# An attention and MoE kernel on one core: dependent operations moved one step back, loads in one ring, a second PSUM bank for P·V

## The chip, the cores and the metric

One core of a Trainium2 chip runs the whole program. The time is the device time of one execution in microseconds (us); the profile is of one further execution.

## The reference

Three stages follow each other. Attention with a decay term is computed for 4 batches of 8 heads, 576 tokens and 64 channels; then a dense layer with a hard-swish gate; then a layer in which each of the 2304 tokens goes to one of 8 experts.

```python
scores = q @ k.T / sqrt(D) + (cum[i] - cum[j])      # cum = cumsum(log f), causal
attn   = softmax(scores);  x = attn @ v             # 4 x 8 x 576 x 64 -> 2304 x 512
h = x @ w_in;  g = h * clip(h + 3, 0, 6) / 6;  x = g @ w_out      # 512 -> 2048 -> 512
e = argmax(x @ w_gate)                               # one of 8 experts per token
out = gate_prob * sigmoid(x @ w_output_gate)[e] * (relu(x @ w1[e]) @ w2[e])   # 512 -> 1024 -> 512
```

## The kernel before

Every matrix product runs as three 16-bit products. An operand is split into a high half (a copy by ACT) and a low half (the difference, by POOL or DVE). So nearly every operand passes an ACT instruction and then a POOL or DVE instruction before TensorE (PE) can use it.

**Attention.** `plan` (L543 to L565) lists the steps of the attention, 37 or 38 in batches 1 to 3. ("p", b, n) prepares a piece n of k and q: `split_kq` (L207) has ACT and POOL split it, SP issues DMA transposes (L269, L285, L288), and a copy of the rows to other partitions (L242 on ACT; L240 on DVE in the first batch) is put off by COPY_LAG scored steps (`copy_rows`, `flush_copies`), or until the step that needs it (`flush_for`). ("v", b, t) prepares a block of v (`prep_v`: ACT L333, POOL L334). The others score a head against a block of queries: `score` (L340: PE L312, then DVE L358 or L384), one step later `soft` (L389: ACT exp L392 and copy L409 or L413, POOL L410 or L415, DMA transpose L421 of the probabilities, tile pt), and LAG = 4 steps later `pv` (L525: PE L444 to L459 into one PSUM bank, tile pv, then `evac` and `evac_last` by DVE L467 to L485 into xs, and ACT and POOL into xn). Two heads share a bank, and the next pair of heads waits until DVE has emptied it. DMA transposes (L507) make xT, the input of the dense layer. The loads of k, q and v have one buffer each (tags ldk, ldq, ldv): those of k and q are issued when the piece before has been split, and that of v inside `prep_v`, just ahead of its use.

**Dense layer.** 6 chunks of 384 tokens. `moe1_steps` (L697) yields 32 parts a chunk: 16 of 12 matmuls into h (L709; then ACT L716, DVE L717, ACT L719, DVE L722, with three PSUM banks in turn), then 4 by 4 parts of 12 matmuls from g (L734; then ACT L743 and DVE L744). The loop over the chunks (L1111) puts attention steps between the parts, by a pace (`want`), so that the attention of later chunks is done beside the dense layer of earlier ones. In this loop the order on PE, ACT and DVE is the order of the program; SP and POOL are ordered by the framework's scheduler.

**Work put between the parts.** The weights of the dense layer arrive as 64-bit floats; `conv_raw` (L661) makes two 16-bit halves of a piece of 512 KB: DVE L672, L674, L676, then ACT L679, then POOL L680. 18 of 32 pieces are converted before the loop, 14 in the first chunk at the parts CONV_AT, and each conversion is followed by `load_next` on SP's queue, for a buffer that the conversion two before it has emptied. Their PSUM bank (ps_cv) is given back after the last of them. `gate_steps` (L792) is the gating of a finished chunk, run from the next chunk's loop at parts 3, 5 and 7. `weights_steps` (L863) converts the first experts' weights (ACT L898, DVE L899) at the even parts of the last two chunks, from `open_weights` on, which first runs the attention to its end. The end of `attn_seq` is one step: `drain(0)` does the last four P·V products and, when it comes to the last unit, that unit's softmax.

**Experts.** From 660 us on the experts run; the diff changes only the order of a few gating steps there.

Of the kernel before, what the change touches and what calls it, by code (L numbers as in the profile page):

```python
# [18 lines left out]
P = 128  # L19
# [12 lines left out]

COPY_LAG = 2

LEAD = 2

LAG = 4
# [23 lines left out]
def attention_moe_kernel(ctx: ExitStack, tc: tile.TileContext, q, k, v, f, w_in, w_out,  # L61
# [112 lines left out]
    def load(i, which):  # L174

        if i >= B * NTB:
            return
        for nm in which:
            with tc.issue_after(gate[0]) if gate else nullcontext():
                if i < (3 if nm == "v" else PE_PIECES):  # L180
                    t = spare(i if nm == "v" else 3 + 2 * i + "kq".index(nm)).bitcast(F32)
                else:
                    t = ap1.tile([P, H * D], F32, tag=f"ld{nm}", name=f"ld{nm}", bufs=1)
                if nm == "v":
                    b, tb = i // NTB, i % NTB
                    r = TBR[tb]
                    src = v[b, :, tb * 128:tb * 128 + r, :].rearrange("h p d -> p h d")
                    for e in range(128 // r):
                        nc.sync.dma_start(out=t[e * r:e * r + r].rearrange("p (h d) -> p h d", d=D), in_=src)
                    t = t.rearrange("p (h d) -> p h d", d=D)  # L190
                else:
                    b, r, hs, (nh, n), cs = piece(i)
                    src = (k if nm == "k" else q)[b, hs, cs, :].rearrange("h (p c) d -> p h (c d)", c=n)
                    nc.sync.dma_start(out=t[0:r].rearrange("p (h x) -> p h x", h=nh), in_=src)
                    t = t.rearrange("p (n d) -> p n d", d=D)
                ld[i, nm] = t

    def load_cum(b, hh):
# [8 lines left out]
    def split_kq(nm, i):  # L207

        b, r, hs, (nh, n), cs = piece(i)
        t = ld.pop((i, nm))  # L210
        p = split_tile(nm, i)
        tv = t[0:r].rearrange("p (h c) d -> p c h d", h=nh) if nm == "k" else t[0:r]
        hi, lo = (p[0:r, :, x] for x in ((0, 1) if nm == "k" else (1, 0)))
        if nm == "k":
            hi, lo = (a.rearrange("p (c h) d -> p c h d", h=nh) for a in (hi, lo))
        nc.scalar.activation(out=hi, in_=tv, func=AF.Copy)
        nc.gpsimd.tensor_tensor(out=lo, in0=tv, in1=hi, op=ALU.subtract)
        return p[0:r].rearrange("p n c d -> p (n c d)")

# [98 lines left out]
    def prep(b, n):  # L318
        i = b * NTB + n
        prep_k(i)  # L320
        if i > 3:
            load(i + 1, "k")
        prep_q(i)
        if i > 3:
            load(i + 1, "q")

    def prep_v(b, tb):
        if b * NTB + tb > 2:
            load(b * NTB + tb, "v")
        assert all(u[1] == b for u in pend)  # L330
        tv, V = ld.pop((b * NTB + tb, "v")), vt[b % len(vt)]
        r = TBR[tb]
        nc.scalar.activation(out=V[:, tb, :, 0:64], in_=tv, func=AF.Copy)  # L333
        nc.gpsimd.tensor_tensor(out=V[0:r, tb, :, 65:129].bitcast(BF16), in0=tv[0:r], in1=V[0:r, tb, :, 0:64],  # L334
                                op=ALU.subtract)


# [173 lines left out]

    cur = {}
    late = []
# [31 lines left out]
    for b in range(B):  # L545
# [19 lines left out]
        ends.append(len(plan) - 1)  # L565
    pend = []
    complete = []

    def attn_seq():

        def drain(n):
            while len(pend) > n:
                u = pend.pop(0)
                if u in unsoft:
                    soft(u)
                    unsoft.remove(u)
                pv(u)

# [25 lines left out]
        for it in plan:  # L604
            if it == "drain":
                drain(0)
                finish(9)
                load(4, "kq")
            elif it[0] == "p":
# [18 lines left out]
            yield "end"  # L628
        drain(0)
        finish(9)  # L630
        yield "end"

# [4 lines left out]
    raws = {}  # L637
    last_act = []
    wof = wo.rearrange("p a b c -> p (a b c)")
# [20 lines left out]

    def conv_raw(nm, i):  # L661

# [15 lines left out]
        tf = t.bitcast(F32).rearrange("p (a b) -> p a b", a=4)  # L678
        last_act.append(nc.scalar.activation(out=hi, in_=tf, func=AF.Copy).ins)  # L679
        nc.gpsimd.tensor_tensor(out=lo.bitcast(BF16), in0=tf, in1=hi, op=ALU.subtract)  # L680

# [110 lines left out]
    def gate_steps(c):  # L792
# [46 lines left out]
        nc.vector.tensor_reduce(out=sx, in_=t2, axis=AX.X, op=ALU.add)  # L839
        nc.scalar.activation(out=z, in_=z, func=AF.Exp, scale=-1.0)  # L840
# [3 lines left out]
        nc.vector.tensor_reduce(out=rank[:, bs].unsqueeze(2), in_=t4, axis=AX.X, op=ALU.add)  # L844
        nc.vector.tensor_scalar(out=z, in0=z, scalar1=1.0, scalar2=None, op0=ALU.add)
        nc.vector.tensor_scalar(out=sx, in0=sx, scalar1=1e-9, scalar2=None, op0=ALU.add)
# [16 lines left out]
    def weights_steps(wp):  # L863
# [28 lines left out]
        for i, (_, e, which, js) in enumerate(parts):  # L892
# [169 lines left out]
    def load_next(queue):  # L1062
        if not loads:
            return
        nm, i = loads[0]

        if ((nm, i - 8) if nm == "wi" else (nm, same_room(i))) in conv:
            return
        loads.pop(0)
        after = gate  # L1070
        with tc.issue_after(after[-1]) if after else nullcontext():
            load_raw(nm, i, queue)
# [23 lines left out]
    goals = [ends[need[c + 1] - 1] + 1 + LAG + XLAG for c in range(NCH - 1)]  # L1096
    mp2 = None
    gq = []
    wg_ = None
# [3 lines left out]
    def open_weights():  # L1103
        nonlocal wp, wg_
        while adv():
            pass
        attn_ctx.close()
        wp = ctx.enter_context(tc.tile_pool(name="wp", bufs=1, side="right"))
        wg_ = weights_steps(wp)

    for c in range(NCH):  # L1111
# [14 lines left out]
        for part in moe1_steps(c):  # L1126
# [9 lines left out]
            while nsteps[0] < want and adv():  # L1136
                pass
            if c == 0 and k_ == GATE_LOAD:
                load_gates()
            if conv and k_ == CONV_AT[2 * NF - EARLY_CONV_DONE - len(conv)]:  # L1140
                assert conv[0] not in loads
                conv_raw(*conv.pop(0))
                load_next(nc.sync)
                if not conv:
                    stage_ctx.close()
                    mp2 = moe1_ctx.enter_context(tc.tile_pool(name="mp2", bufs=1))
                    setup_gates()
            if gq and k_ in (3, 5, 7):
                run(gq[0])
                if k_ == 7:  # L1150
                    run(gq.pop(0))
            if c == NCH - 2 and wp is None and len(complete) == 3 * B:
# [19 lines left out]
        gq.append(gate_steps(c))  # L1172
    run(wg_, 4 * KD + 1 - nw)
    main.close()
    ET = mybir.EngineType
# [6 lines left out]
    run(first[0], 2)  # L1182
    run(last, 2)
    run(first[0], 3)
    run(last, 2)
    count_rounds()
# [100 lines left out]
```

## Time and profile before

| | |
|---|---|
| median of 3 runs | 891.51 us |
| lowest and highest | 888.04 and 895.68 us |
| the profiled execution | 894.32 us, its span 892.6 us |
| mean granted TensorE clock | 0.935 |

The time of a row is counted from the start of the span. Idle time of an engine stands in brackets with what ended it, its releaser. The granted clock is a share of 2.4 GHz; the lower level is 1.2 GHz, so a stretch with a mean of 0.75 was at the lower level half of the time. SPq rows are DMA issues by SP; their duration is that of the issue, not of the transfer.

### The profile page before, as it was taken

How to read it: one execution, taken by the hardware profiler on the slowest of the kernel's cores; microseconds unless marked ns; L12 is line 12 of the kernel's file. 1: busy time of each engine (PE TensorE's matmuls, PEld its weight loads, DVE VectorE, ACT ScalarE, POOL GpSimd, SP SyncE). 2: the span in 40 equal slices, each digit the busy share in tenths (PEclk: the TensorE clock that was granted, in tenths of full speed). 3: DMA queues.
4: the chain of work that ended last, by engine and by line, in shares of the span. 5: the costliest groups of instructions: out<-in, count | busy, mean ns of one | idle time of the engine just before them, and what ended most of it. 6: DMA issues, size and time to landing. Idle time of an engine off the chain costs nothing. (4 is left out here: it accounts for less than half of the span.)

```text
span 892.6 us, 16737 instructions
## 1 busy us (share of the span) xinstructions
PE 749.2 (84%) x6177; PEld 481.4 (54%) x6177; DVE 460.9 (52%) x1272; ACT 456.4 (51%) x909; POOL 306.5 (34%) x388
## 2 busy tenths in 40 slices
PE   4744696666999989997799897976999999999994
PEld 3532354343566556664456554643576866766651
DVE  7896866343754364357333861467232455554510
ACT  4854566553776576457555762444011455554520
POOL 8345545552454344343344441000003222221011
PEclk9967898897999999999899997999899999999997
DMA  9558477784668777477448564532325699887410
GB/s 250 152 172 184 108 115 159 163 165 101 137 116 146 131 122 145 89 138 128 95 90 152 90 110 127 174 109 95 95 59 144 145 262 264 272 268 227 156 47 35
DMA packets 263778, 127.95 MB, mean 143 GB/s; under 512 B 214658, under 2 KB 247522, under 8 KB 263684
## 3 DMA queue, kind: packets, MB, share of 16 engines
q1 hardware_dynamic: 258724, 111.00, 55.7%
q0 software_dynamic: 4960, 15.73, 5.1%
q8 instruction: 54, 0.88, 0.4%
q14 instruction: 40, 0.33, 0.1%
HBM read 71.52 MB, written 10.08 MB: 91 GB/s over the span
## 5 line engine op out<-in xcount | busy, mean ns | idle before, releaser
L709 PE MATMUL mm<-xT,wi 128*128 128x384 f16 (+1 forms) x1152 | 211.6, 339 | 29.3 <-DVE g L722 16.5
L734 PE MATMUL mm<-g,wo 128*128 128x384 f16 (+1 forms) x1152 | 208.5, 342 | 10.5 <-ACT wo L679 9.3
L709 PEld LDWEIGHTS <-wi 128*128 128x128 f16 (+1 forms) x1152 | 112.9, 101 | 106.3 <-issue 44.0
L734 PEld LDWEIGHTS <-wo 128*128 128x128 f16 (+1 forms) x1152 | 114.6, 102 | 90.7 <-issue 14.0
L410 POOL TENSOR_TENSOR pn<-ms,pn 128x384 bf16<-128x384 f32 (+1 forms) x80 | 80.9, 1011 | 99.3 <-ACT pn L409 41.3
L899 DVE TENSOR_TENSOR W<-stw,W 128x1024 bf16<-128x1024 f32 x64 | 77.6, 1224 | 58.8 <-ACT W L898 48.1
L996 PEld LDWEIGHTS <-W 128*128 128x128 f16 (+1 forms) x1344 | 99.3, 98 | 13.4 <-issue 5.4
L996 PE MATMUL mm<-xs,W 128*128 128x256 f16 (+3 forms) x1152 | 97.0, 246 | 3.4 <-issue 1.3
L1015 PE MATMUL mm<-W,hT 128*128 128x512 f16 (+1 forms) x432 | 94.4, 379 | 0.6 <-PEq L1224 0.2
L898 ACT ACTIVATE W<-stw 128x1024 f16<-128x1024 f32 x64 | 66.4, 1052 | 36.2 <-DMA stw<-in_moe_w_dram 33.7
L358 DVE CUSTOM_DVE_ANT_1 ms<-sc,mask 128x128 f32<-128x128 f32 (+3 forms) x128 | 59.6, 486 | 46.3 <-PE sc L312 41.3
L717 DVE SCALAR_TENSOR_TENSOR mm<-hr,mm 128x384 f32<-128x384 f32 x96 | 53.7, 560 | 55.1 <-ACT hr L716 54.9
L392 ACT ACTIVATE ms<-ms,nm 128x512 f32<-128x512 f32 (+3 forms) x144 | 79.7, 576 | 4.5 <-DVE nm L358 3.0
L444 PE MATMUL pv<-vt,pt 128*128 128x65 f16 x320 | 42.1, 201 | 42.3 <-DVE xs L485 15.2
L716 ACT ACTIVATE hr<-mm,bias 128x384 f32<-128x384 f32 x96 | 55.1, 574 | 31.3 <-PE mm L709 31.1
L1015 PEld LDWEIGHTS <-hT 128*128 128x128 f16 (+1 forms) x432 | 41.9, 98 | 50.9 <-issue 1.6
L722 DVE TENSOR_TENSOR g<-mm,g 128x384 bf16<-128x384 f32 x96 | 53.3, 555 | 30.0 <-ACT g L719 29.5
L744 DVE SCALAR_TENSOR_TENSOR x<-mm,x 128x384 bf16<-128x384 f32 x24 | 13.4, 558 | 96.4 <-ACT x L743 96.4
L719 ACT ACTIVATE g<-mm 128x384 f16<-128x384 f32 x96 | 45.9, 478 | 30.0 <-DVE mm L717 29.5
L1000 DVE SCALAR_TENSOR_TENSOR hT<-mm,hT 128x128 bf16<-128x128 f32 (+1 forms) x96 | 31.8, 354 | 49.1 <-ACT hT L999 47.6
L312 PE MATMUL sc<-K,Q 67*128 67x128 f16 (+2 forms) x192 | 47.5, 303 | 9.9 <-ACT Q L242 7.3
L743 ACT ACTIVATE x<-mm 128x384 f16<-128x384 f32 x24 | 11.7, 489 | 85.5 <-PE mm L734 85.4
(183 smaller groups left out, 1109.9 us busy)
## 6 DMA issues: line engine op xcount, KB each, us to landing
stw<-in_moe_w_dram SPq DMA_DIRECT2D x64, 512.0 KB
wo<-in_moe_w_in_dram SPq DMA_DIRECT2D x16, 512.0 KB
raw<-in_moe_w_out_dram SPq DMA_DIRECT2D x13, 512.0 KB
rows<-rw POOLq DMA_DIRECT2D x15, 256.0 KB, 2.6
ldv<-in_v_dram SPq DMA_DIRECT2D x13, 256.0 KB
ldk<-in_k_dram SPq DMA_DIRECT2D x12, 256.0 KB
ldq<-in_q_dram SPq DMA_DIRECT2D x12, 256.0 KB
g<-in_moe_w_out_dram SPq DMA_DIRECT2D x3, 512.0 KB
```

Of the source, the lines that this page charges most:

```text
L358: nc.vector.tensor_tensor_reduce(out=pairs(ms[:, off:off + w]), in0=ps[:, 0:w].rearrange("p (c j) -> p c j", c=2), in1=pairs(mask[:, 640 - ...
L392: nc.scalar.activation(out=ms[:, off:off + w], in_=ms[:, off:off + w], func=AF.Exp, scale=-1.0, bias=nm[:, i:i + 1])
L410: nc.gpsimd.tensor_tensor(out=lo.bitcast(BF16), in0=ms[:, 0:N], in1=hi, op=ALU.subtract)
L709: nc.tensor.matmul(ps[:, 0:w], lhsT=l.bitcast(BF16) if a else l, rhs=r.bitcast(BF16) if b2 else r, start=i == 0, stop=i == 3 * KD - 1)
L716: nc.scalar.activation(out=hr, in_=pw, func=AF.Relu, bias=bias3)
L717: nc.vector.scalar_tensor_tensor(out=pw, in0=hr, scalar=6.0, in1=pw, op0=ALU.min, op1=ALU.mult)
L722: nc.vector.tensor_tensor(out=g[:, m, 1, 0:w].bitcast(BF16), in0=pw, in1=g[:, m, 0, 0:w], op=ALU.subtract)
L734: nc.tensor.matmul(ps[:, 0:w], lhsT=l.bitcast(BF16) if a else l, rhs=r.bitcast(BF16) if b2 else r, start=i == 0, stop=i == 3 * NF - 1)
L898: nc.scalar.activation(out=hi, in_=sts[i], func=AF.Copy)
L899: nc.vector.tensor_tensor(out=lo.bitcast(BF16), in0=sts[i], in1=hi, op=ALU.subtract)
L996: nc.tensor.matmul(ps[:, 0:w], lhsT=l.bitcast(BF16) if a else l, rhs=r.bitcast(BF16) if b2 else r, start=i == 0, stop=i == 3 * KD - 1)
L1015: nc.tensor.matmul(ps, lhsT=l.bitcast(BF16) if a else l, rhs=r.bitcast(BF16) if b2 else r, start=i == 0, stop=i == 3 * NF2 - 1)
```

## The change

Eight edits, here in their core.

1. One tag "ld" with three buffers takes the loads of k, q and v in the order of use (`coming`); each split of a piece and each `prep_v` issues the next load.
2. COPY_LAG goes from 2 to 1, and in batches 1 to 3 the k and q pieces stand earlier and the later v blocks later in the plan.
3. In the end of the attention all open softmax steps come first, and the last P·V products are spread over steps of their own.
4. `conv_raw` in the loop leaves its ACT and POOL half to the next part, and the load that follows is issued by ACT instead of SP.
5. P·V takes a second PSUM bank (ps_x, in the place of ps_cv) in turn with the first, once the conversions are done.
6. In `gate_steps` both Exp instructions of ACT come one part later.
7. In `weights_steps` DVE's half (L899) and the next load come one part after ACT's half.
8. After the loop the gating steps of the last chunk are called in other numbers, to fit 6.

```diff
-COPY_LAG = 2
+COPY_LAG = 1
 def load(i, which):
-                    t = ap1.tile([P, H * D], F32, tag=f"ld{nm}", name=f"ld{nm}", bufs=1)
+                    t = ap1.tile([P, H * D], F32, tag="ld", name="ld", bufs=3)
+    def load_ahead():
+        if coming:
+            load(*coming.pop(0))
 def split_kq(nm, i):
         nc.gpsimd.tensor_tensor(out=lo, in0=tv, in1=hi, op=ALU.subtract)
+        load_ahead()
 def prep(b, n):
         prep_k(i)
-        if i > 3:
-            load(i + 1, "k")
         prep_q(i)
-        if i > 3:
-            load(i + 1, "q")
 def prep_v(b, tb):
-        if b * NTB + tb > 2:
-            load(b * NTB + tb, "v")
...
+        if b * NTB + tb > 2:
+            load_ahead()
 def pv(u):
-                cur["o"] = ps_pv.tile([P, 512], F32, tag="pv", name="pv")
+                second = ps_x and cur["pool"] is ps_pv
+                cur["pool"] = ps_x if second else ps_pv
+                cur["o"] = cur["pool"].tile([P, 512], F32, tag="px" if second else "pv", name="pv")
-            plan += [("p", b, 1)] + ga[0:4] + [("v", b, 0), ("v", b, 1), ga[4], ("p", b, 2), ga[5], ga[6], ("v", b, 2), ga[7]]
+            plan += [("p", b, 1)] + ga[0:3] + [("p", b, 2), ga[3], ("v", b, 0), ("v", b, 1), ga[4], ga[5], ("p", b, 3),
+                                              ga[6], ga[7]]
-            plan += [gc[0], ("p", b, 3)] + gc[1:4] + [("v", b, 3), gc[4], ("p", b, 4), gc[5], ("v", b, 4), gc[6], gc[7]]
+            plan += [gc[0], ("v", b, 2), gc[1], gc[2], ("p", b, 4), gc[3], gc[4], ("v", b, 3), gc[5], gc[6],
+                     ("v", b, 4), gc[7]]
 def attn_seq():
         def drain(n):
+            while unsoft and (unsoft[0] is not pend[-1] or n < LAG):
+                soft(unsoft.pop(0))
             while len(pend) > n:
-                u = pend.pop(0)
-                if u in unsoft:
-                    soft(u)
-                    unsoft.remove(u)
-                pv(u)
+                pv(pend.pop(0))
...
-        drain(0)
-        finish(9)
-        yield "end"
+        while unsoft:
+            soft(unsoft.pop(0))
+        for n in range(LAG, -1, -1):
+            drain(n)
+            finish(1)
+            yield "end"
+        while late:
+            finish(1)
+            yield "end"
 def gate_steps(c):
-        nc.scalar.activation(out=t2, in_=t2, func=AF.Exp)
...
+        yield
+        nc.scalar.activation(out=t2, in_=t2, func=AF.Exp)
         yield
 def weights_steps(wp):
             nc.scalar.activation(out=hi, in_=sts[i], func=AF.Copy)
-            nc.vector.tensor_tensor(out=lo.bitcast(BF16), in0=sts[i], in1=hi, op=ALU.subtract)
-            if len(sts) < len(parts):
-                fetch()
+            def rest(lo=lo, st=sts[i], hi=hi):
+                nc.vector.tensor_tensor(out=lo.bitcast(BF16), in0=st, in1=hi, op=ALU.subtract)
+                if len(sts) < len(parts):
+                    fetch()
+            if wlo is None:
+                rest()
+            else:
+                wlo.append(rest)
             yield
 for part in moe1_steps(c):
+            for split in late_steps:
+                split()
+                load_next(nc.scalar)
+            late_steps.clear()
+            for lo in wlo:
+                lo()
+            wlo.clear()
             if conv and k_ == CONV_AT[2 * NF - EARLY_CONV_DONE - len(conv)]:
-                conv_raw(*conv.pop(0))
-                load_next(nc.sync)
+                late_steps.append(conv_raw(*conv.pop(0), later=True))
-            if gq and k_ in (3, 5, 7):
+            if gq and k_ in (3, 5, 6, 7, 8, 9):
```

## Rows read from the trace of the kernel before

**Rows 1.** The page's first part: busy us, share of the span, instructions of each engine.

```profile
PE 749.2 (84%) x6177; PEld 481.4 (54%) x6177; DVE 460.9 (52%) x1272; ACT 456.4 (51%) x909; POOL 306.5 (34%) x388
```

**Rows 2.** Stretches: length, busy (count) of PE, PEld, DVE, ACT, POOL, clock, DMA, GB/s.

```profile
75.00:217.00 142.00, 99.46 (x719) 58.08 (x719) 79.27 (x207) 77.07 (x154) 70.99 (x79) 0.85 0.66 135
217.00:550.00 333.00, 302.82 (x2656) 192.35 (x2655) 170.99 (x589) 208.47 (x430) 142.90 (x182) 0.96 0.64 118
550.00:650.00 100.00, 83.61 (x517) 48.57 (x516) 48.65 (x120) 34.14 (x55) 3.81 (x5) 0.93 0.41 127
650.00:893.00 243.00, 224.94 (x1971) 154.21 (x1968) 98.86 (x204) 95.12 (x184) 46.58 (x45) 0.98 0.60 172
```

**Rows 3.** PE's waits, 75 to 217 us: line, releaser: us in total, times, longest.

```profile
PE pv L444 <- DVE xs L485: 11.6, 3, 5.5
PE mm L734 <- ACT wo L679: 9.3, 2, 6.4
PE pv L444 <- DVE xs L469: 5.4, 2, 3.8
PE pv L444 <- ACT vt L333: 5.1, 1, 5.1
PE sc L312 <- DVE Q L240: 2.6, 1, 2.6
PE sc L312 <- ACT Q L242: 1.8, 1, 1.8
```

**Rows 4.** PE's waits, 217 to 550 us.

```profile
PE sc L312 <- ACT Q L242: 5.5, 3, 3.3
PE pv L456 <- DMA pt<-pn: 5.5, 1, 5.5
PE pv L444 <- ACT vt L333: 4.9, 2, 4.3
PE pv L444 <- DMA pt<-pn: 3.7, 2, 2.5
PE pv L444 <- DVE xs L485: 3.6, 2, 1.9
PE mm L709 <- DVE g L722: 3.0, 5, 0.9
PE pv L445 <- POOL vt L334: 2.0, 2, 1.0
PE pv L444 <- DVE xs L469: 1.6, 2, 0.9
```

**Rows 5.** PE's waits, 550 to 650 us.

```profile
PE mm L709 <- DVE g L722: 11.8, 6, 2.6
PE mm L936 <- DVE R L958: 2.8, 1, 2.8
PE mm L936 <- DVE g L722: 1.5, 1, 1.5
```

**Rows 6.** The stretch from 202 to 210 us, columns as in rows 2.

```profile
202.00:210.00 8.00, 4.20 (x12) 1.47 (x12) 2.51 (x4) 0.63 (x1) 1.15 (x1) 0.57 0.60 140
```

**Rows 7.** Timeline at 437 us: ACT's half of a block of v.

```profile
437.08 0.64 ACT L333 ACTIVATE vt<-ldv 128x512 f16<-128x512 f32 x1 [4.54 <-DMA ldv<-in_v_dram]
```

**Rows 8.** Timeline at 197 and 201 us: load of a raw piece, and its conversion.

```profile
196.91 0.53 SPq L658 DMA_DIRECT2D raw<-in_moe_w_out_dram  x1
201.19 0.69 DVE L672 TENSOR_SCALAR cv<-raw 128x512 int32<-128x512 int32 x1 [5.62 <-DMA raw<-in_moe_w_out_dram]
```

**Rows 9.** Timeline at 106 us: ACT's half of a conversion.

```profile
106.51 0.63 ACT L679 ACTIVATE wo<-w 128x512 f16<-128x512 f32 x1 [2.08 <-DVE w L676]
```

**Rows 10.** Timeline at 594 us, last chunk: DVE's half of an expert's weight.

```profile
594.40 1.23 DVE L899 TENSOR_TENSOR W<-stw,W 128x1024 bf16<-128x1024 f32 x1 [1.50 <-ACT W L898]
```

**Rows 11.** Timeline at 191 to 197 us: transposes of a piece of q, its copy.

```profile
190.68 2.57 SPq L288 DMA_TRANSPOSE q<-qp  x2
197.07 1.05 ACT L242 ACTIVATE Q<-q 64x1024 f16<-64x1024 f16 x1
```

More of the change, by code (lines that the diff above doesn't have):

```diff
@@ L174, in load @@
     def load(i, which):
-        if i >= B * NTB:
-            return
         for nm in which:
@@ L510, in xtrans @@
             done += n
-    cur = {}
+    cur = {"pool": None}
+    ps_x = None
     late = []
@@ L565, in attention_moe_kernel @@
         ends.append(len(plan) - 1)
+    coming = []
+    for it in plan[plan.index("drain") + 1:]:
+        if it[0] in "pv" and len(it) == 3:
+            coming += [(it[1] * NTB + it[2], nm) for nm in ("kq" if it[0] == "p" else "v")]
     pend = []
@@ L607, in attn_seq @@
                 finish(9)
-                load(4, "kq")
+                for _ in range(3):
+                    load_ahead()
             elif it[0] == "p":
@@ L637, in attention_moe_kernel @@
     raws = {}
-    last_act = []
     wof = wo.rearrange("p a b c -> p (a b c)")
@@ L659, in load_raw, with conv_raw @@
         raws[nm, i] = raw
-    def conv_raw(nm, i):
+    def conv_raw(nm, i, later=False):
         if nm == "wi":
@@ L678, in conv_raw, with split @@
         tf = t.bitcast(F32).rearrange("p (a b) -> p a b", a=4)
-        last_act.append(nc.scalar.activation(out=hi, in_=tf, func=AF.Copy).ins)
-        nc.gpsimd.tensor_tensor(out=lo.bitcast(BF16), in0=tf, in1=hi, op=ALU.subtract)
+        def split():
+            nc.scalar.activation(out=hi, in_=tf, func=AF.Copy)
+            nc.gpsimd.tensor_tensor(out=lo.bitcast(BF16), in0=tf, in1=hi, op=ALU.subtract)
+        if not later:
+            split()
+        return split
     w_in_w = w_in.bitcast(I32).rearrange("(k p) f -> p k f", p=P)
@@ L839, in gate_steps @@
         nc.vector.tensor_reduce(out=sx, in_=t2, axis=AX.X, op=ALU.add)
-        nc.scalar.activation(out=z, in_=z, func=AF.Exp, scale=-1.0)
         t4 = sm("t4", E)
@@ L844, in gate_steps @@
         nc.vector.tensor_reduce(out=rank[:, bs].unsqueeze(2), in_=t4, axis=AX.X, op=ALU.add)
+        yield
+        nc.scalar.activation(out=z, in_=z, func=AF.Exp, scale=-1.0)
+        yield
         nc.vector.tensor_scalar(out=z, in0=z, scalar1=1.0, scalar2=None, op0=ALU.add)
@@ L1069, in load_next @@
         loads.pop(0)
-        after = gate
-        with tc.issue_after(after[-1]) if after else nullcontext():
+        with tc.issue_after(gate[-1]) if gate and queue is nc.sync else nullcontext():
             load_raw(nm, i, queue)
@@ L1097, in attention_moe_kernel @@
     mp2 = None
+    px_ctx = ctx.enter_context(ExitStack())
+    late_steps, wlo = [], []
     gq = []
@@ L1103, in open_weights @@
     def open_weights():
-        nonlocal wp, wg_
+        nonlocal wp, wg_, ps_x
         while adv():
             pass
+        px_ctx.close()
+        ps_x = None
         attn_ctx.close()
@@ L1137, in attention_moe_kernel @@
                 pass
+            for split in late_steps:
+                split()
+                load_next(nc.scalar)
[3 more added lines that the diff above has]
+            wlo.clear()
             if c == 0 and k_ == GATE_LOAD:
@@ L1141, in attention_moe_kernel @@
                 assert conv[0] not in loads
-                conv_raw(*conv.pop(0))
-                load_next(nc.sync)
[L1144 to L1147, printed above, removed]
-            if gq and k_ in (3, 5, 7):
+                late_steps.append(conv_raw(*conv.pop(0), later=True))
+            elif not conv and mp2 is None:
+                stage_ctx.close()
+                mp2 = moe1_ctx.enter_context(tc.tile_pool(name="mp2", bufs=1))
+                ps_x = px_ctx.enter_context(tc.tile_pool(name="ps_x", bufs=1, space=PSUM))
+                setup_gates()
+            if gq and k_ in (3, 5, 6, 7, 8, 9):
                 run(gq[0])
-                if k_ == 7:
-                    run(gq.pop(0))
+                if k_ == 9:
+                    gq.pop(0)
             if c == NCH - 2 and wp is None and len(complete) == 3 * B:
@@ L1173, in attention_moe_kernel @@
     run(wg_, 4 * KD + 1 - nw)
+    for lo in wlo:
+        lo()
+    wlo = None
     main.close()
@@ L1182, in attention_moe_kernel @@
     run(first[0], 2)
-    run(last, 2)
+    run(last, 3)
     run(first[0], 3)
-    run(last, 2)
+    run(last, 4)
     count_rounds()
```

## Prediction

> **What bounds the kernel now.** I read the shares of the engines, then the stretches by stage, then PE's waits in each stretch, then single timelines. PE is busy for 84% of the span and no other engine for more than 52% [rows 1], so the question is where PE stands still. The stretches show the stages: start of the attention to 75 us, first chunk of the dense layer (75 to 217), chunks 2 to 5 with the rest of the attention (217 to 550), the last chunk with the experts' first weights (550 to 650), the experts. From 75 to 650 PE idles 142.0 − 99.5 = 42.5, 333.0 − 302.8 = 30.2 and 100.0 − 83.6 = 16.4 us, 89 us in all [rows 2]. These waits have many releasers [rows 3 to 5]: DVE that has not emptied a PSUM bank, ACT that has not copied, a DMA that was late. None of these engines is full; each wait is one of order, a producer placed just before its consumer on an engine that runs its instructions one after the other.
>
> The waits cost twice. In the three stretches the granted clock is 0.85, 0.96 and 0.93 of 2.4 GHz [rows 2], and it falls after PE has stood still: in the 8 us from 202 to 210, in which a wait of 6.4 us ended [rows 3], it was 0.57, while PE worked for 4.2 us [rows 6]. Since the lower level, 1.2 GHz, is half, PE works at it for about 2 × (0.15 × 99.5 + 0.04 × 302.8 + 0.07 × 83.6) = 66 us, and half of that, 33 us, is lost.
>
> The experts' stretch has 18 us of PE idle, most of it at its very end; the diff changes only the order of small gating steps in it, so I cost it at nothing, ±2 us. The start to 75 us, and PE's wait there for the first xT, stand before or beside the edits and are left as they are, ±3 us.
>
> **The change part by part**, as PE idle that goes.
>
> 1. *Loads of v in the ring.* ACT stood 4.54 us for a load of v that was issued at its use [rows 7], and everything behind it on ACT stood too. PE's waits for vt are 5.1 + 4.9 + 2.0 = 12.0 us [rows 3, 4]. In the ring a load goes out three loads ahead, several steps of over 2 us. 11 go. SP's issue of the load now waits for POOL's half of the piece just split; behind it stand that piece's transposes, which wait for the same POOL instruction, and transposes of probabilities that POOL makes later. What is new for them is the 0.5 us of one issue.
> 2. *Row copies.* The copies stood just ahead of the step that needs them: 1.8 + 5.5 = 7.3 us for Q from ACT, 2.6 from DVE [rows 3, 4]. With the pieces earlier in the plan and the copies due one scored step sooner, parts of the dense layer lie between copy and use. 7 and 1 go.
> 3. *Raw loads from ACT's queue.* DVE stood 5.62 us for a piece whose load SP had issued only 4.3 us before (196.91 to 201.19) [rows 8], and there are three such waits. PE paid 9.3 us for wo, and 3.8 us at the PSUM bank (the longest of the two xs L469 waits) [rows 3]. ACT would issue the load one part after the conversion that frees the buffer, some 10 us sooner. What is late next is ACT's and POOL's half of the last piece, two parts ahead of its use. 11 of 13.1 go.
> 4. *ACT's half of a conversion one part later.* ACT stood 2.08 us in front of that copy, and it held back L716, for which DVE waited before it emptied the PV bank [rows 9]. DVE's own 2.1 us of conversion stay in the chain, and the second bank isn't there in this stretch. The bounds are 0 and 13.2 us, all of the bank waits there but the 3.8 [rows 3]; I take the length of the ACT copy, 0.65 us, four times: 2.6.
> 5. *The end of the attention.* The last unit's softmax came when all else was done, and PE waited 5.5 us for its transpose [rows 4]. Now it starts before the last products, which lie between parts. 5 go.
> 6. *Second PV bank*, from the second chunk on: 3.6 + 1.6 = 5.2 us there [rows 4]; 4.5 go.
> 7. *Weights in the last chunk.* DVE stood 1.50 us for ACT's half [rows 10] and PE then waited for L722, 11.8 + 2.8 + 1.5 = 16.1 us in all [rows 5]. With its half a part later DVE does not stand. Three waits lose 1.5 each; of the others, where DVE also makes one-hot rows and is nearly full, I take 2 together. 6.5 go.
> 8. *Gating Exp one part later*: the waits for L722 and pt in the middle stretch, 3.0 + 3.7 = 6.7 us [rows 4], lie partly behind that Exp on ACT; bounds 0 and 6.7, I take 2.5.
>
> Sum: 11 + 8 + 11 + 2.6 + 5 + 4.5 + 6.5 + 2.5 = 51.1 us of 89. The same share (0.57) of the clock's 33 us is 19. Together 70.
>
> Against it stand new costs. Nine loads issued by ACT at 0.53 us [rows 8] take 4.8 us of ACT, which has half its time free; bounds 0 and 4.8, taken 1. A row copy due a step earlier can reach ACT before its transposes have landed: in the trace two transposes of q were issued from 190.68 to 193.25 and the copy ran at 197.07 [rows 11]; one scored step of some 4 us sooner it would come at 193, and stand some 2 us until the data is there, with L716 behind it on ACT. Three PSUM banks in L709 hide most of that; for 12 pairs of copies the bounds are 0 and 48, taken 4. At four places two conversions follow each other in consecutive parts, and the second's L676 now waits for POOL's half of the first: bounds 0 and 8, taken 2. Together 7. And where a wait goes, the next producer comes out a little behind it, above all DVE's and ACT's chain through L716 to L722, so I keep a fifth of the 70, 14 us.
>
> 70 − 14 − 7 = 49. The profiled execution took 894.3 us, 2.8 above the median of 891.5; 894.3 − 49 − 2.8 = **842 us**.
>
> The Trainium skill, "DMA: Bandwidth & Descriptors", section "Issuing engines are not separate DMA queues", says that DMAs issued by several engines share the same 16 DMA engines, so that spreading them only saves issue time. By it part 3 would save ACT's and SP's half microseconds and no more, which is the second rival below; no row here shows a load from ACT's queue.
>
> **The rivals.** *The waits change hands.* ACT and DVE are near 60% in the middle stretch (208 and 171 of 333 us) [rows 2] and work in bursts; each removed wait may show the next one. If half of the 70 comes back and the costs double to 14: 894.3 − 35 + 14 − 2.8 = 870. Against it: the waits are few and long, and each has one releaser.
>
> *The raw loads come no sooner.* If a load that shares the DMA engines with the transposes takes over 2.3 us longer than the 4.3 us of [rows 8], DVE stands again. Part 3's 11 and its clock share of 4 are lost, four fifths of which I had counted: 854.
>
> *Slower.* The copies due a step sooner stop ACT in front of transposes that have not landed. The place is L242; the price is 4 us each for 12 pairs, with 2 us of low clock after each: 842 + 72 = 914. It decides once ACT stands over 3 us at each pair (then the 49 us are used up). For it speaks the margin of −2 us worked out above and one more load ahead of the transposes on SP; against it that ACT's part can wait while PE works in 12 matmuls ahead.
>
> *It does not do what it says.* The sum of waits may be only the visible side of one chain per step (scores, DVE, ACT, POOL, transpose, product), so that the same time goes to other names: 886.
>
> **How the numbers follow.** Forecast 0.60, change of hands 0.20, raw loads 0.08, slower 0.06, no effect 0.06. Without the fifth and the costs the time would be 894.3 − 70 − 2.8 = 821, and with a little more of part 4, 818: the low end. The high end is 874, just above the first rival. About 0.06 lies below and 0.13 above. A measurement of this kernel tells about 1% from no change. Faster by over 1% (below 882.6): 0.60 + 0.08 + nearly all of 0.20, 0.87; within 1%: 0.07; slower: 0.06.
>
> **What would show it.** Right: ACT's waits for ldv and DVE's for raw are gone, PE's waits for vt, wo and Q are under 3 us each, pt no longer has a 5.5 us wait, the bank waits after the first chunk are under 1 us, the last chunk's waits for L722 are near 1 us each, and the clock from 217 to 550 is 0.98 or more; PE's idle from 75 to 650 is near 50 us. Wrong: new idle of ACT before L242, of DVE before L676 behind POOL or before raw, of PE at the end of chunk 5 for xT of the last chunk (its attention now ends some five parts later), or waits of the same sum under other names.

## The result and the profile after

The changed kernel takes 849.44 us (median of 4 runs, 845.84 to 851.13) against 891.79 of the kernel before beside it: ratio 0.952, 95% interval 0.947 to 0.957. The forecast was 842.0, its range 818 to 874. A second measurement (label again, below) gave 847.62 and 0.951 (0.947 to 0.954).

The stages end earlier now. These are the stretches of both kernels by their own boundaries (first matmul of the dense layer, of chunk 2, of the last chunk, of the experts); the columns are those of [rows 2]: length, then busy time and count of PE, PEld, DVE, ACT, POOL, then granted clock, DMA share, GB/s. First before:

```profile
75.92:216.75 140.83, 99.21 (x718) 57.89 (x717) 78.47 (x206) 76.82 (x154) 70.75 (x78) 0.85 0.66 134
216.75:572.68 355.93, 325.75 (x2801) 206.17 (x2798) 179.91 (x598) 215.60 (x439) 142.90 (x182) 0.97 0.64 124
572.68:660.78 88.10, 71.71 (x444) 41.40 (x442) 40.44 (x112) 27.75 (x48) 3.81 (x5) 0.92 0.31 90
660.78:892.60 231.82, 214.16 (x1905) 147.75 (x1902) 98.30 (x203) 94.62 (x183) 46.58 (x45) 0.98 0.63 181
```

Then the changed kernel:

```profile
75.50:203.98 128.48, 95.97 (x718) 56.74 (x718) 81.22 (x209) 79.67 (x158) 73.14 (x80) 0.88 0.76 151
203.98:537.07 333.09, 320.86 (x2795) 205.10 (x2795) 171.79 (x592) 210.37 (x432) 142.21 (x181) 0.98 0.65 126
537.07:615.87 78.80, 67.40 (x445) 39.75 (x443) 43.95 (x115) 30.61 (x51) 3.81 (x5) 0.98 0.41 122
615.87:847.30 231.43, 214.10 (x1904) 147.96 (x1902) 98.21 (x203) 95.18 (x183) 48.74 (x45) 0.98 0.63 181
```

The span fell by 45.3 us: 12.3 in the first chunk, 22.8 in chunks 2 to 5, 9.3 in the last chunk, 0.8 in the start and the experts together. In the three stretches PE's idle (length less PE busy) fell from 41.6 + 30.2 + 16.4 = 88.2 to 32.5 + 12.2 + 11.4 = 56.1, so by 32.1 us; PE's busy time for the same matmuls fell by 3.2 + 4.9 + 4.3 = 12.4, and the granted clock rose in each. In sum over the three stretches the work of DVE (298.8 us before, 297.0 after) and of ACT (320.2 and 320.7) is the same as before.

PE's waits in the first chunk of the changed kernel, as in [rows 3] (releaser, sum, times, longest; the 12.3 of xT ended as the stretch began; left out are 2.7 for pt, 1.0 for q, 0.8 for ACT's half of wo and 0.4 for ACT's of vt):

```profile
PE mm L727 <- DMA xT<-xn: 13.3, 2, 12.3
PE pv L444 <- DVE xs L485: 8.9, 3, 5.2
PE mm L727 <- DVE g L740: 6.3, 1, 6.3
PE pv L444 <- DVE xs L469: 4.6, 2, 3.0
PE sc L316 <- DVE Q L244: 3.0, 1, 3.0
...
PE mm L752 <- POOL wo L695: 2.0, 3, 0.7
PE pv L445 <- POOL vt L332: 1.6, 1, 1.6
```

In chunks 2 to 5, as in [rows 4] (left out are 0.8 for ACT's half of vt and 0.7 for pt):

```profile
PE mm L727 <- DVE g L740: 4.5, 6, 1.8
PE mm L727 <- DVE lg L834: 3.6, 1, 3.6
PE pv L445 <- POOL vt L332: 2.6, 3, 1.0
PE mm L727 <- DMA xT<-xn: 1.0, 1, 1.0
```

In the last chunk, as in [rows 5] (left out are 1.0 and 0.6 for the gating's banks):

```profile
PE mm L727 <- DVE g L740: 6.5, 5, 1.9
PE mm L963 <- DVE g L740: 3.1, 1, 3.1
```

Gone are the 7.3 us for ACT's copies of Q, the 5.5 for pt, and the bank waits after the first chunk. The waits for vt stand at 5.4 instead of 13.0 (2.0 in the first chunk with ACT's 0.4, 3.4 later with ACT's 0.8), those for wo at 2.8 instead of 10.4; [rows 3] leaves out the 1.0 and 1.1 of these that were for POOL in the first chunk. New are 6.3 for g at 102 us (1.7 in the first chunk before) and 3.6 for a gating bank at 310.

### The profile page after: what moved, and what is told of

The parts are those of the page before. It is cut to its first block, busy times and chain, and to the rows that moved or that the text cites. A ratio compares the mean times of both kernels' runs of the same rounds, so it can differ in the third digit from the quotient of the medians.

```text
span 847.3 us, 16712 instructions
## 1 busy us (share of the span) xinstructions
PE 736.1 (87%) x6177; PEld 478.1 (56%) x6177; DVE 458.1 (54%) x1272; ACT 457.2 (54%) x909; POOL 309.0 (36%) x388
## 5 line engine op out<-in xcount | busy, mean ns | idle before, releaser
L752 PE MATMUL mm<-g,wo 128*128 128x384 f16 (+1 forms) x1152 | 198.2, 329 | 2.9 <-POOL wo L695 2.0
L752 PEld LDWEIGHTS <-wo 128*128 128x128 f16 (+1 forms) x1152 | 110.6, 99 | 75.5 <-issue 3.3
L922 DVE TENSOR_TENSOR W<-stw,W 128x1024 bf16<-128x1024 f32 x64 | 77.5, 1222 | 45.3 <-ACT W L919 30.9
L358 DVE CUSTOM_DVE_ANT_1 ms<-sc,mask 128x128 f32<-128x128 f32 (+3 forms) x128 | 59.5, 485 | 32.1 <-PE sc L316 28.5
L734 ACT ACTIVATE hr<-mm,bias 128x384 f32<-128x384 f32 x96 | 55.3, 576 | 27.4 <-PE mm L727 27.0
L740 DVE TENSOR_TENSOR g<-mm,g 128x384 bf16<-128x384 f32 x96 | 53.2, 554 | 23.4 <-ACT g L737 22.8
L1027 DVE SCALAR_TENSOR_TENSOR hT<-mm,hT 128x128 bf16<-128x128 f32 (+1 forms) x96 | 32.1, 354 | 53.0 <-ACT hT L1026 40.5
L1049 POOL DMA_INDIRECT out_dram<-y,ids x18 | 20.7, 1152 | 96.6 <-ACT y L1048 56.8
```

The lines of the kernel that those rows point to most:

```text
L358: nc.vector.tensor_tensor_reduce(out=pairs(ms[:, off:off + w]), in0=ps[:, 0:w].rearrange("p (c j) -> p c j", c=2), in1=pairs(mask[:, 640 - ...
L734: nc.scalar.activation(out=hr, in_=pw, func=AF.Relu, bias=bias3)
L740: nc.vector.tensor_tensor(out=g[:, m, 1, 0:w].bitcast(BF16), in0=pw, in1=g[:, m, 0, 0:w], op=ALU.subtract)
L752: nc.tensor.matmul(ps[:, 0:w], lhsT=l.bitcast(BF16) if a else l, rhs=r.bitcast(BF16) if b2 else r, start=i == 0, stop=i == 3 * NF - 1)
L922: nc.vector.tensor_tensor(out=lo.bitcast(BF16), in0=st, in1=hi, op=ALU.subtract)
```

## The experiments

Each experiment undoes one part of the changed kernel, or adds to it; prices are against the changed kernel, as difference of the ratios to before times 892 us, from the mean ratio of its two measurements (0.9512). A ratio's interval is about ±0.003, some 3 us, and a price is the difference of two, so one under some 4 us is not told from none. Of the prices below, those of the loads (8 us) and of the expert weights (10 us) are clear, and that of the raw loads (4.3) just so; all others lie under that bound, and for them only the waits in the traces can speak.

**The changed kernel again.** The same code.

> The changed kernel itself once more, as the measure for the others: 847 to 851 us, ratio to before 0.950 to 0.955. Its first chunk may differ from 128.5 us by some 3 us: kernels whose first chunk has the same code had 124.8 (the weights' order undone), 125.8 (the attention's end undone) and 126.4 us (one bank for PV).

847.62 us, ratio 0.9505 (0.9469 to 0.9540). The first chunk took 123.1 us with nearly the same waits of PE (idle 30.9 instead of 32.5), at a granted clock of 0.92 instead of 0.88. So the first chunk varies by 5 us from one execution to the next, most of it by its clock. In four kernels below that have the same code there (one bank for PV, the weights, the attention's end, the Exp), PE's idle in it was 31.9, 30.6, 29.9 and 27.7 us. One profile can't tell differences of 5 us in this stretch.

**Copies due two steps later again.**

```diff
-COPY_LAG = 1
+COPY_LAG = 2
```

> The changed kernel with COPY_LAG back at 2 (row copies due one scored step later; the earlier pieces of the plan stay). Theory 1 (the copy a step sooner is what costs: the profile after has ACT stand 1.14 + 1.67 us in front of L246 ahead of PE's 3.59 us wait at 310, and 2.38 + 1.11 us at 177 ahead of a 2.96 us bank wait at 187): ACT's waits at L246 (6.2 us in the first chunk, 5.8 in the middle) fall under 3 us together, both PE waits go, and the time is 3 to 10 us below the changed kernel's 849.4. Rival (the earlier due time is needed, as part 2 of the prediction has it): PE's waits for Q from ACT come back, 7.3 us as in rows 3 and 4, and the time is 853 to 860.

847.02 us, 0.9492 (0.9461 to 0.9523): not slower, 1.8 us faster if anything, just above theory 1's range (839 to 846) and not told from none. The traces tell more than the time: no wait for Q from ACT comes back, ACT's waits at L246 are down from 12.0 to 0.9 us, the wait at 187 is 1.6 us instead of 3.0, and the 3.6 us wait is gone. But PE's idle in chunks 2 to 5 is 13.2 us, beside 12.2 in the changed kernel, since other waits got longer (for pt, g and the gating): that the shorter lag costs time is not shown, only that it isn't needed. How the 3.6 us arose in the changed kernel is seen on the timelines of ACT, DVE and PE (start, length, instruction, in brackets the idle time ahead and its releaser):

```profile
305.33 1.06 ACT L246 ACTIVATE K<-K 64x1024 f16<-64x1024 f16 x1 [1.14 <-DMA K<-kp]
308.05 1.05 ACT L246 ACTIVATE Q<-q 64x1024 f16<-64x1024 f16 x1 [1.67 <-DMA q<-qp]
309.13 0.58 ACT L734 ACTIVATE hr<-mm,bias 128x384 f32<-128x384 f32 x1
```

```profile
309.74 0.56 DVE L735 SCALAR_TENSOR_TENSOR mm<-hr,mm 128x384 f32<-128x384 f32 x1 [5.63 <-ACT hr L734]
310.21 0.20 DVE L834 COPY lg<-mm 128x48 f32<-128x48 f32 x1
```

```profile
310.47 1.78 PE L727 MATMUL mm<-xT,wi 128*128 128x384 f16 x5 [3.59 <-DVE lg L834]
```

ACT stands for two transposes, L734 stands behind it, DVE behind L734, and the gating's PSUM bank behind DVE. This is the third rival's mechanism, at the place that the prediction named; PE paid for it plainly once, not twelve times. In the ten profiles of kernels with COPY_LAG 1 the wait is there, 1.0 to 6.7 us long; in the three of changed kernels with COPY_LAG 2 it is not.

**Part 2 undone as a whole**: the plan of before with COPY_LAG 2.

```diff
-COPY_LAG = 1
+COPY_LAG = 2
-            plan += [("p", b, 1)] + ga[0:3] + [("p", b, 2), ga[3], ("v", b, 0), ("v", b, 1), ga[4], ga[5], ("p", b, 3),
-                                              ga[6], ga[7]]
+            plan += [("p", b, 1)] + ga[0:4] + [("v", b, 0), ("v", b, 1), ga[4], ("p", b, 2), ga[5], ga[6], ("v", b, 2), ga[7]]
...
```

> The changed kernel with the whole of part 2 undone: the plan of before (pieces of k, q and v nearer to their use) and COPY_LAG 2; the ring stays. Beside it stands the kernel that undoes the lag alone (847.0). Theory 1 (the pieces' earlier place is what takes PE's waits for Q, 7.3 us, and part of those for vt): these waits return, PE's for Q from ACT 6 us or more, the time is 855 to 862. Rival (the ring's early loads alone make the pieces come in time): waits for Q under 3 us, time 846 to 851.

851.91 us, 0.9529 (0.9499 to 0.9559): between the two theories in time, some 3 us above the kernel that has only the lag undone and not told from it. The waits are theory 1's: PE waits 1.7 + 5.5 = 7.2 us for Q from ACT again (first chunk, then chunks 2 to 5). So the pieces' earlier place removed them, and the shorter lag wasn't needed for it.

```profile
PE sc L316 <- ACT Q L246: 1.7, 1, 1.7
...
PE sc L316 <- ACT Q L246: 5.5, 3, 2.6
```

**Loads as before**: three single buffers, v loaded at its use.

```diff
-                    t = ap1.tile([P, H * D], F32, tag="ld", name="ld", bufs=3)
+                    t = ap1.tile([P, H * D], F32, tag=f"ld{nm}", name=f"ld{nm}", bufs=1)
...
+        if b * NTB + tb > 2:
+            load(b * NTB + tb, "v")
```

> The changed kernel with the loads of k, q and v as before: one buffer for each of the three, v loaded at its use, k and q right after the piece before is split. Theory 1 (part 1 of the prediction, 11 us of waits with their clock share): ACT stands again some 4 us for each load of v, PE's waits for vt go from 5.4 us in both stretches to 12 or more, the time is 858 to 865. Rival (the pieces' earlier place in the plan already gives the cover, the ring is worth little): PE's waits for vt under 8 us, time 848 to 853.

856.38 us, 0.9600 (0.9573 to 0.9628): 8 us slower, nearer to theory 1. ACT stands 22.8 us for seven loads of v, and PE's waits for vt are 6.4 us in the first chunk and 12.3 later, more than before the change. ACT's waits over chunks 1 to 5, then PE's in chunks 2 to 5:

```profile
ACT vt L338 <- DMA ldv<-in_v_dram: 22.8, 7, 6.6
```

```profile
PE pv L451 <- ACT vt L338: 9.3, 3, 4.5
...
PE pv L452 <- POOL vt L339: 3.0, 3, 1.0
```

**Raw loads back on SP.**

```diff
             for split in late_steps:
                 split()
-                load_next(nc.scalar)
...
                 late_steps.append(conv_raw(*conv.pop(0), later=True))
+                load_next(nc.sync)
```

> The changed kernel with the late raw loads back on SP, issued right after the conversion that frees their room (ACT issues none). Theory 1 (part 3 of the prediction: on SP the loads stand behind transposes that wait for POOL, so they come too late): DVE's waits for raw in the first chunk go from 2.9 us back above 8, PE's waits for wo from 2.8 above 6, first chunk 5 to 10 us longer than 128.5, time 854 to 860. Rival (the raw loads come no sooner from ACT's queue than from SP's, as all share the DMA engines; ACT's issues lie behind its own waits): DVE's waits for raw stay under 4 us, first chunk within 2 us of 128.5, time 847 to 851.

855.91 us, 0.9560 (0.9530 to 0.9590): 4 us slower, theory 1's time. DVE's waits for raw are 8.2 us, one of them 7.56, as it said. But PE pays for it at the PV bank (10.5 us at L469 instead of 4.6), not at wo (1.5), and the first chunk took 130.7 us, 2 longer than 128.5 and not 5 to 10. PE's idle in it is 33.1 us, beside 32.5 and 30.9 in the changed kernel, as other waits got shorter: the trace shows the mechanism, and 0.6 to 2.2 us of its price. SP's queue, DVE and PE of this kernel:

```profile
157.89 1.22 SPq L421 DMA_TRANSPOSE pt<-pn  x1
159.21 0.53 SPq L192 DMA_DIRECT2D ld<-in_q_dram  x1
159.78 2.56 SPq L507 DMA_TRANSPOSE xT<-xn  x2
162.44 0.53 SPq L187 DMA_DIRECT2D ld<-in_v_dram  x1
163.07 0.56 SPq L671 DMA_DIRECT2D raw<-in_moe_w_out_dram  x1
```

```profile
155.99 0.69 DVE L689 SCALAR_TENSOR_TENSOR w<-raw,cv 128x512 int32<-128x512 int32 x1
...
167.88 0.69 DVE L685 TENSOR_SCALAR cv<-raw 128x512 int32<-128x512 int32 x1 [7.56 <-DMA raw<-in_moe_w_out_dram]
```

```profile
171.54 0.21 PE L444 MATMUL pv<-vt,pt 128*128 128x65 f16 x1 [6.75 <-DVE xs L469]
```

The room was free when L689 ended at 156.7; SP came to the load at 163.07; from 157.89 on it had issued a transpose of pt, the two of xT and two other loads, one right behind the other. In the changed kernel ACT issued the same load at 158.21, as L689 of that conversion ended, and DVE waited 0.49 us:

```profile
158.21 0.44 ACTq L671 DMA_DIRECT2D raw<-in_moe_w_out_dram  x1
```

```profile
157.48 0.69 DVE L689 SCALAR_TENSOR_TENSOR w<-raw,cv 128x512 int32<-128x512 int32 x1
...
162.29 0.70 DVE L685 TENSOR_SCALAR cv<-raw 128x512 int32<-128x512 int32 x1 [0.49 <-DMA raw<-in_moe_w_out_dram]
```

From issue to use it took 4.8 us on SP's queue and 4.1 on ACT's. The transfer did not become much faster; it started sooner after its room came free.

**ACT's and POOL's half at once.**

```diff
-                late_steps.append(conv_raw(*conv.pop(0), later=True))
+                late_steps.append(conv_raw(*conv.pop(0)) and (lambda: None))
```

> The changed kernel with ACT's and POOL's halves of a conversion in the same part as DVE's again; the raw load still goes out from ACT a part later. Theory 1 (part 4 of the prediction, 2.6 us with its clock share some 3): ACT's waits for DVE's words at L694 go from 10 us in the first chunk to over 30, time 851 to 854. Rival 1 (the later split also makes DVE stand at L689, 19 us in the first chunk, and gives back what it brings): L689's waits fall under 5 us, time 847 to 850. Rival 2 (the bank waits of the first chunk, 13.5 us, hang on the split's place wholly, the upper bound of part 4): time above 858.

853.18 us, 0.9550 (0.9527 to 0.9574): 3.4 us slower, theory 1's time, but not told from none. ACT's wait for DVE's words in the first chunk rises from 9.5 us, seven times, to:

```profile
ACT wo L694 <- DVE w L689: 25.9, 15, 2.5
```

DVE's waits at L689 fall from 19 to 7.1 us. That ACT's order is what costs the 3.4 us is not shown: PE's idle in the first chunk is 28.8 us, less than the 32.5 and 30.9 of the changed kernel, and what grew is the wait for the gating's bank at 310 us (6.5 instead of 3.6), where ACT stood 4.06 us for a transpose of K (1.14 in the changed kernel) and no conversion runs any more.

**A second buffer for the words.**

```diff
-        t = stp.tile([P, WL // 4], I32, tag="w32", name="w32", bufs=1)
+        t = m_all.bitcast(I32) if later and len(conv) % 2 else stp.tile([P, WL // 4], I32, tag="w32", name="w32", bufs=1)
...
-    M = const.tile([P, NB, NV, E], BF16, name="M")
+    M = (m_all := const.tile([P, 1024], BF16, name="M"))[:, 0:NB * NV * E].rearrange("p (n v e) -> p n v e", v=NV, e=E)
```

> The changed kernel with a second buffer for the converted words (every other late conversion writes into the room of M, which is not used before the gating). Theory 1 (with the split a part later DVE stands in front of L689 for POOL's half of the conversion before, 11.8 + 7.2 us in the first chunk, and the bank wait of 2.96 us at 187 and part of the 5.22 us at 142 hang on it): L689's waits for POOL fall under 6 us (the early conversions keep theirs), the first chunk is 3 to 6 us shorter than 128.5, the time 844 to 847. Rival (DVE's stand is slack, and the bank waits hang on the single PV bank and on L487's copies): first chunk within 1.5 us of 128.5, time 848 to 851.

848.97 us, 0.9507 (0.9473 to 0.9541): the rival's time. L689's waits for POOL fell from 19.0 to 8.6 us, more than half, and nothing came of it that the time shows. The first chunk took 124.7 us, with 28.3 us of PE idle; the unchanged code also took 123.1 to 128.5, with 27.7 to 32.5.

**One bank for PV.**

```diff
-                ps_x = px_ctx.enter_context(tc.tile_pool(name="ps_x", bufs=1, space=PSUM))
```

> The changed kernel without the second PSUM bank for PV. Theory 1 (part 6 of the prediction, 4.5 us with its clock share some 6): PE waits again for the bank (L469, L485) for 5 us from chunk 2 on, the stretch of chunks 2 to 5 goes from 333.1 to 338 to 341 us, time 854 to 858. Rival (the bank was late only because DVE was held up by ACT's late halves, and these edits alone clear it): the bank waits there under 1.5 us, time within 2 us of the changed kernel's 849.4.

850.95 us, 0.9549 (0.9523 to 0.9576): the rival's, in the time and in what PE waits. In chunks 2 to 5 a single bank wait came back, of 5.2 us before:

```profile
PE pv L444 <- DVE xs L469: 1.2, 1, 1.2
```

The other edits had cleared the rest; which of them is not shown. The 3 us by the ratios are not told from none, and the trace names no wait for them.

**DVE's half of the expert weights at once.**

```diff
-            if wlo is None:
+            if wlo is None or True:
```

> The changed kernel with DVE's half of an expert weight in the same part as ACT's half again. Theory 1 (part 7 of the prediction, 6.5 us with its clock share 8): DVE stands 1.5 us for ACT before each L922, PE's waits for g in the last chunk go from 9.6 us (6.5 + 3.1) to 14 to 16, that chunk from 78.8 to 84 to 87 us, time 854 to 858. Rival (the last chunk is bound by how much DVE has to do, 44 of 79 us with one-hot rows in bursts, not by the order): the last chunk under 80.5 us, time 848 to 851.

858.12 us, 0.9627 (0.9601 to 0.9654): 10 us slower, theory 1's time, the largest price of all. The last chunk, then DVE's and PE's waits in it:

```profile
535.84:622.95 87.11, 69.37 (x445) 40.62 (x443) 44.06 (x115) 30.41 (x51) 3.82 (x5) 0.94 0.38 109
```

```profile
DVE W L922 <- ACT W L919: 13.4, 11, 1.6
```

```profile
PE mm L727 <- DVE g L740: 11.4, 7, 2.6
```

DVE's waits for ACT's half were 1.0 us in the changed kernel. DVE has the same 44 us to do in both; only the order differs, and with it 8.3 us of the chunk.

**The attention's end as before.**

```diff
-        while unsoft:
-            soft(unsoft.pop(0))
-        for n in range(LAG, -1, -1):
-            drain(n)
-            finish(1)
-            yield "end"
-        while late:
-            finish(1)
-            yield "end"
+        drain(0)
+        finish(9)
+        yield "end"
```

> The changed kernel with the attention's end as before: all products still open drained at once, the last softmax among them. Theory 1 (part 5 of the prediction): PE waits 5 to 6 us for the last transpose of probabilities at the end of chunk 5, with the low clock after it 6 to 8 us in all, time 855 to 858; the last chunk of the dense layer may start with a lower granted clock, as before (0.92 against 0.98). Rival (with the weights' loads and the last xT later by the five parts over which the attention now ends, the old end costs no more than it brings): time 848 to 851.

852.29 us, 0.9553 (0.9527 to 0.9579): 3.7 us slower, between the two and not told from none. PE's waits for pt in chunks 2 to 5 are 4.2 us (2.2 and three of 0.9 or less) instead of 0.7, and chunk 5 takes 84.7 us instead of 79.3.

**The gating's Exp at once**, in four steps a chunk.

```diff
-            if gq and k_ in (3, 5, 6, 7, 8, 9):
+            if gq and k_ in (3, 5, 7):
...
```

> The changed kernel with the gating's Exp in the same part as the DVE steps ahead of it, in four steps as before. Theory 1 (part 8 of the prediction, 2.5 us with its clock share 3): ACT stands in front of the two Exps in each chunk for 6 us in all, PE's waits for g from chunk 2 to 5 go from 4.5 us to 7, time 852 to 854. Rival (ACT has room there, the 3.6 us at the gating's PSUM bank come from the row copies and stay): time 847 to 851, and the PE waits of that stretch within 1.5 us of 13.

849.76 us, 0.9510 (0.9481 to 0.9540): the rival's time. ACT stands 5.4 us for the Exps as theory 1 had it, and PE's waits for g rise from 4.5 to 5.1 only. The rival's waits did not come either: that at the gating's bank grew to 6.7 us, as ACT stood 4.21 us for a transpose of K, and PE's waits of that stretch to 17 instead of 13, without an effect on the time that can be measured.

**Second buffer and later copies together.**

```diff
-COPY_LAG = 1
+COPY_LAG = 2
...
-        t = stp.tile([P, WL // 4], I32, tag="w32", name="w32", bufs=1)
+        t = m_all.bitcast(I32) if later and len(conv) % 2 else stp.tile([P, WL // 4], I32, tag="w32", name="w32", bufs=1)
...
```

> Both edits that the traces suggest together: a second buffer for the converted words and COPY_LAG 2. Theory 1 (the changed kernel pays for two of its own edits: ACT stands some 12 us at L246, DVE 16 us at L689 behind POOL): both waits go, PE idles under 25 us in the first chunk and under 11 in chunks 2 to 5, the time is 842 to 846, below both kernels. Rival (each gain was given back elsewhere when tried alone, 847.0 and 849.0, and the clock falls after other waits): 846 to 849.

845.09 us, 0.9463 (0.9432 to 0.9494), beside the changed kernel's 847.62 on the same chip. The time is theory 1's, but neither PE's idle is nor all of the waits (DVE still stands 7.7 us at L689, early conversions included, and ACT 3.5 at L246): 28.5 us in the first chunk and 13.1 in chunks 2 to 5, not under 25 and 11. In chunks 2 to 5 the granted clock was 1.00. The two intervals overlap, so that this kernel beats the changed one is likely and not shown; that it beats the one before is.

## Why the prediction was right, and where it was off

The forecast was 49 us less for the profiled execution, and then 2.8 more off, because before's profiled execution lay that much above its median. The span fell by 45.3 us; the changed kernel's profiled execution lay near its own median, so the 2.8 did not come. That makes 6.5 of the 7.4 us that were missing.

The parts of the 49: idle was to fall by 51.1 less a fifth, less 7 of new costs, so 34; it fell by 32.1. The clock was to give 19 less a fifth, 15; it gave 12.4. The kept fifth ("the next producer comes out a little behind") and the clock's share were thus of the right size together. By the names, some 43 us of waits went, where 51.1 were forecast, and some 12 came elsewhere (10 of them named below, 2 for xT). The mechanism held: late producers were moved, and PE's waits for them fell. Which edit is worth what did not hold for most terms, and that their errors cancelled so nearly is luck. By single terms:

- *Loads in the ring*: forecast 11 of 12.0; 7.6 of 13.0 went. ACT's waits for v nearly went (2.1 of 13.7 us left), as said; but 5.4 us for vt stay, most of them in the products' first use of a block whose POOL half has just been done. What failed is the assumption that the load was all of that wait. Undone it costs 8 us.
- *Row copies*: 7.3 us for Q from ACT went, as said; the step that failed is to credit them to both edits. The plan's order did it. The lag took no wait that a trace shows and brought ACT's 12 us at L246, whose price is not told from none; and of DVE's 2.6 us nothing went (3.0 now, last section).
- *Raw loads*: DVE's waits went from 17.1 to 2.9 us and those for wo from 10.4 to 2.8, as said. But the price of SP's queue alone is 4 us, not 12. With the loads on SP and all else changed, wo is on time all the same; the kernel with all of part 2 undone has 6.7 us for wo back in its one profile, so the plan's order seems to hold part of that term. And of the 3.8 us at the bank that the term took in, 2.96 stayed (at 187 us) although the raw loads were on time: that wait was not theirs. In the rows the same load began 6.4 us after its room was free on SP and at once on ACT. By the Trainium skill ("DMA: Bandwidth & Descriptors", section "Issuing engines are not separate DMA queues") issuing from several engines saves only the time that the sequencer takes to initiate a DMA. The rows agree in kind, not with the half microsecond that the prediction made of it: the load stood behind the issues of all that was ahead of it on SP (a transpose of pt, 1.22 us, two of xT, 2.56, and two loads, 0.53 each), and these were saved.
- *Late half of the conversion*: forecast 2.6; the price of 3.4 is not told from none, and PE's idle in the first chunk does not bear it out, so this term stays open. Its cost was sized at 2 us (bound 8); DVE stood 19 us at L689 instead. With the second buffer 10 us of that went without a gain in time, so most of it was slack. Not all of it need be: ahead of the 6.3 us for g at 102 us DVE stood 2.4, 0.5 and 0.5 us there, in three conversions one behind the other, and that wait is 3.2 us with the halves at once and 3.5 with COPY_LAG 2.
- *End of the attention*: forecast 5 of 5.5; the wait went, the price is 3.7, not told from none.
- *Second bank*: forecast 4.5 of 5.2. The waits went, but 4 of the 5.2 us also go without the bank. Here the mechanism failed: the other edits had brought DVE to the bank in time.
- *Weights in the last chunk*: forecast 6.5 of 16.1; PE's waits there fell to 11.2, by 5, and the chunk by 9.3 with its clock (0.92 to 0.98). Undone: 10 us. This was the best-founded term, and it has the largest price.
- *Exp*: forecast 2.5; not found.

The prices of the undone parts sum to about 34 us (8 + 1.5 for part 2 + 4 + 3.4 + 3.7 + 3.3 + 10 − 0.2) of 43.5. The 9 us between them may be gains that come only with several edits together; but eight prices of some ±4 us each leave that open.

The rivals: waits did change hands, the first rival, but for some 10 us (g 4.6 more at 102 us and 1.5 more later, 3.6 at the gating's bank), not for 35. The raw loads came sooner. The slower rival's mechanism exists, and its cost is too small to be measured. Of the signs named, PE's idle from 75 to 650 near 50, under 3 us for vt and 1 us for each wait in the last chunk were missed (58.6 in the same window; 5.4; five of 1.3 on average and one of 3.1). Two signs of a wrong forecast came, ACT's idle ahead of L246 and DVE's ahead of L689 behind POOL, and did not decide it.

## What to carry to other kernels

When no engine is full and PE's waits have many releasers, price the producer's place in its engine's order: one dependent instruction moved a part later was worth 10 us in the last chunk, and loads issued ahead of their use 8, while a second word buffer and a second bank were worth nothing that could be measured once the order was right. Before you move a consumer of a DMA earlier on an engine that others queue behind, look at what it will stand for: the copies due a step sooner made ACT stand 12 us and took no wait from PE. Undo each part alone: the sum of waits by name told which would go, but not which edit would take them.

## What the runs showed of the hardware

**These 16-bit copies on DVE end only behind POOL's running instruction.** In the kernel before the two row copies of 64x512 took 0.39 and 0.29 us:

```profile
87.65 0.39 DVE L240 COPY K2t<-K1t 64x512 f16<-64x512 f16 x1
88.07 0.29 DVE L240 COPY Q<-q 64x512 f16<-64x512 f16 x1
```

In the changed one, due sooner, they meet POOL's work. DVE, then POOL:

```profile
85.92 1.05 DVE L244 COPY K2t<-K1t 64x512 f16<-64x512 f16 x1
87.00 1.13 DVE L244 COPY Q<-q 64x512 f16<-64x512 f16 x1
```

```profile
85.66 1.15 POOL L695 TENSOR_TENSOR wi<-w,wi 128x512 bf16<-128x512 f32 x1 [1.09 <-ACT wi L694]
86.78 1.20 POOL L410 TENSOR_TENSOR pn<-ms,pn 128x512 bf16<-128x512 f32 x1
```

In the kernel with COPY_LAG 2 the first copy falls into a gap of POOL and the second does not:

```profile
88.44 0.28 DVE L244 COPY K2t<-K1t 64x512 f16<-64x512 f16 x1
88.75 1.25 DVE L244 COPY Q<-q 64x512 f16<-64x512 f16 x1
```

```profile
87.16 1.16 POOL L410 TENSOR_TENSOR pn<-ms,pn 128x512 bf16<-128x512 f32 x1
88.69 1.15 POOL L410 TENSOR_TENSOR pn<-ms,pn 128x512 bf16<-128x512 f32 x1 [0.37 <-ACT pn L409]
```

Each slow copy ends 0.2 us or less after the POOL instruction that was running as it began. The Trainium skill, "SBUF — State Buffer", section "Who interferes with whom", says that a copy on DVE can run in a mode that takes, for the whole instruction, a pair of ports shared with GpSimd (POOL here), and that whichever of the two issues second blocks until the first is through. These rows agree (0.28 us beside no POOL instruction, 1.05 to 1.25 beside one); that the copies ran in such a mode no row names. PE's 2.6 us for DVE's copies became 3.0. With copies of 0.39 and 0.29 us from 85.92 on, PE's wait, which ended at 88.18, would have ended at some 86.6, an estimate from these rows, and so have been 1.5 us, near the 1.6 that the prediction left of it.

**The same wait does not always cost clock.** Both profiles of the changed kernel have the same wait of PE in the last chunk, 3.11 and 3.10 us for g (L963), with the granted clock at 1.00 up to it and PE busy for 2.7 of the 4 us ahead of it. In the 6 us behind it the clock was 0.72 in the first, so that 6 × 0.28 = 1.7 us were lost, and 1.00 in the second:

```profile
582.09:588.09 6.00, 5.84 (x37) 3.08 (x37) 4.92 (x16) 2.38 (x3) 2.17 (x2) 0.72 0.46 139
```

```profile
579.46:585.46 6.00, 5.83 (x47) 3.61 (x47) 4.92 (x16) 2.38 (x3) 2.17 (x2) 1.00 0.48 139
```

A few us of clock are thus not to be had by counting waits, and one profile of a kernel says little below 5 us.
